# Narrow attention products set singly between feed-forward products, with three other moves in the hand-made order

## The chip, the core and the metric

The kernel runs on one core of one Trainium2 chip. The metric is the device time of one execution in microseconds (us); before the change the median of three runs is 494.69 us (491.87 to 498.25). Engines: PE multiplies matrices (PEld is its weight loading), DVE, ACT and POOL work element by element, SP issues most of the DMA transfers.

## The reference, cut to what matters

For each of 4 batches and 8 heads a recurrent attention runs over 768 positions with 40 values a head; all heads' outputs then go through a feed-forward of 320 -> 2048 -> 320 with a softplus between:

```
C = f*C + i * outer(v, k);  n = f*n + i*k
y = sigmoid(o) * (C @ q) / max(|n . q|, 1)
x = y, all heads of a position side by side      # 3072 x 320
out = softplus(x @ w_in) @ w_out
```

The kernel computes the recurrence in chunks of 128 positions: inside a chunk by products of queries, keys and values, across chunks by the state C and n.

## The kernel before, in words

**Tiles and steps.** 24 steps, one per (batch, chunk), make 8 tiles of 384 positions. The first tile holds chunk 0 of batches 1, 2, 0; the second, the steps (3,0), (0,1) and (0,2); the third, (0,3), (0,4), (0,5). Steps of the first two tiles take the plain way (`plain_step`, L752), the others the wide one (`wide_step`, L804), which sends its result through memory and is not changed.

**Feed-forward.** A block is one slice of 128 of the 2048 hidden columns for one tile: eight products into `hp` (L974, 384 columns), softplus on ACT twice (L848, L849), a difference on DVE (L852), and, two blocks later, nine products into `po` (L942, 320 columns). Blocks 0 to 9 of the first tile come first, then the 16 of the second tile, the last 6 of the first, and the other tiles.

**A plain step.** `scores` (L499) multiplies keys and queries into `sp`, two halves of four heads, and DVE multiplies each by the decays `pw` (L506), which it has scanned (L430) from `fb`, loaded by SP (L421). `inter` (L525) multiplies queries with the old state into `ip`, 8 products of 42 columns, one a head; DVE scales that into `y1` (L531). `values` (L535) multiplies the weighted scores with the values into `yp`, 8 products of 41 columns; DVE adds and divides (L542 to L550) into `x`. `split_x` (L609) transposes `x` on PE into `xp`, ACT casts it into the tile's `X` (L619), and DVE writes the remainder (L621). `state` (L477) makes `cp`, and `new_state` adds it to the state (L486). `ip`, `yp`, `sp`, `xp`, `cp` and the gates' `pg` share one pool of two PSUM buffers (`ps_a`, tag `pa`); a third tile waits until a buffer is read out.

**Gates.** `later_gates` (L142) computes all later chunks' gates once; `pg` (L173) holds their transposes, which ACT copies into `gT` (L179, L180).

**Weights.** Each tensor's chunk is loaded by SP (L221 to L227) into one of three buffers `wr`, brought to float32 by two ACT and two DVE operations (`single`, L190), cast by ACT into the high part (`wih` L236, `woh` L251) and subtracted by POOL into the low part (`wil` L243, `wol` L253). The `wr` buffers also take the queries and keys of every second wide tile (`prepare`, L267).

**Order.** `products` (L923) emits the feed-forward product by product and counts them with `n`; `tick(n)` resumes every generator whose time has come. A generator yields either a time relative to its base, or, below -1000, a distance to the last resumption; `rel` turns a yield of r into such a distance. Engines run their own instructions strictly in the order so written.

Of the kernel before, what the change touches and what calls it, by code (L numbers as in the profile page):

```python
# [39 lines left out]
def mlstm_moe_kernel(  # L40
# [96 lines left out]
        nc.scalar.copy(gT[:, 0, 0, :], pg)  # L137
        yield

    GR = [4, 9, 8, 16, 21, 27]  # L140

    def later_gates():  # L142

        w = S - L
        ig = p1.tile([NCHAIN, w], F32, tag="hiq", name="ig")
        fg = p1.tile([NCHAIN, w], F32, tag="hik", name="fg")
        nc.sync.dma_start(fg, gates[0, :, L:])
        nc.sync.dma_start(ig, gates[1, :, L:])
        yield GR[0]
        m = p2.tile([NCHAIN, w + 1], F32, tag="eg", name="m")  # L150
        nc.vector.tensor_copy(m[:, 0:1], m_end)
        nc.vector.tensor_tensor_scan(m[:, 1:], fg, ig, m[:, 0:1], ALU.add, ALU.max)
        yield GR[0]
        nc.gpsimd.tensor_tensor(fg, fg, m[:, 0:w], op=ALU.add)
        nc.gpsimd.tensor_tensor(fg, fg, m[:, 1:], op=ALU.subtract)
        nc.gpsimd.tensor_tensor(ig, ig, m[:, 1:], op=ALU.subtract)
        yield GR[1]
        nc.scalar.activation(fg, fg, AF.Exp)
        nc.scalar.activation(ig, ig, AF.Exp)
        yield GR[2]  # L160
        d1 = p1.tile([NCHAIN, w], F32, tag="loq", name="d1")
        nc.gpsimd.memset(d1, 0.0)

        nc.vector.tensor_copy(d1[:, 0:w:L], fg[:, 0:w:L])
        nc.vector.memset(fg[:, 0:w:L], 0.0)
        nc.sync.dma_start(fz_d[1:].rearrange("c p s -> p c s"), fg.rearrange("p (c s) -> p c s", s=L))
        fc = d1
        nc.vector.tensor_tensor_scan(fc, fg, d1, 0.0, ALU.mult, ALU.add)
        nc.vector.tensor_copy(fl_s[:, 1:], fc[:, L - 1 : w : L])
        yield GR[3]  # L170
        nc.sync.dma_start(fl_d[:, 1:], fl_s[:, 1:])
        nc.sync.dma_start(fc_d[1:].rearrange("c p s -> p c s"), fc.rearrange("p (c s) -> p c s", s=L))
        pg = ps_a.tile([128, NC + NI - 2, NCHAIN], F32, tag="pa", name="pg")  # L173
        for c in range(1, NC):
            nc.tensor.transpose(pg[:, c - 1], ig[:, (c - 1) * L : c * L], ident[:NCHAIN, :NCHAIN])
        for c in range(1, NI):
            nc.tensor.transpose(pg[:, NC + c - 2], fc[:, (c - 1) * L : c * L], ident[:NCHAIN, :NCHAIN])
        yield GR[4]
        nc.scalar.copy(gT[:, 0, 1:], pg[:, 0 : NC - 1])  # L179
        nc.scalar.copy(gT[:, 1, 1:NI], pg[:, NC - 1 :])  # L180
        yield GR[5]
        nc.sync.dma_start(flast[:, :, 1:], fl_d[:, 1:].partition_broadcast(D))


    wih = cpool.tile([128, 3, DFF], F32R, name="wih")
# [62 lines left out]
    def weights_out(u):  # L248
# [11 lines left out]
        -48, -34, -64, -8, 19, 8, 4, 6, 14, 17, 31, 47, 50, 62, -12, 68, 79, 107, 139,  # L260
    )
    N_LOAD, N_FB, N_SCAN, N_CN, N_VW, N_SIG, N_SP0, N_SP1, N_CP, N_CD, N_IP, N_VI, N_YP, N_X, N_XP = (
        -20, -22, 8, 26, 12, 12, 12, 22, 40, 44, 45, 30, 46, 60, 80,
    )
    OF = [0, 8]

    def prepare(t):  # L267

        yield 0
        parts[t] = []  # L270
        for nm, src in zip("qk", qk[t]):
            lo = (
                stage.tile([D3, H, L], F32R, tag="wr", bufs=WB, name=f"lo{nm}{t}")
                if t % 2
                else p1.tile([D3, H, L], F32R, tag=f"lo{nm}", name=f"lo{nm}{t}")
            )
            nc.sync.dma_start(lo.bitcast(F32), src)
            parts[t].append([lo])
        yield PRD[t > WIDE]
        for (lo,), nm in zip(parts[t], "qk"):  # L280
            hi = p1.tile([D3, H, L], F32R, tag=f"hi{nm}", name=f"hi{nm}{t}")
            nc.scalar.copy(hi, lo.bitcast(F32))
            parts[t]["qk".index(nm)] = hi, lo
            yield -1000 - 5
        for hi, lo in parts[t]:
            for h in range(0, H, 4):
                h2 = slice(h, h + 4)
                nc.gpsimd.tensor_tensor(lo[:, h2], lo[:, h2].bitcast(F32), hi[:, h2], op=ALU.subtract)
                yield -1000 - PSY[t > WIDE]

    PRD, PSY = [40, 78], [8, 12]

    parts = {}
    Xs = {}
# [230 lines left out]
    def inter(z):  # L525
        ip = ps_a.tile([128, H, E2], F32, tag="pa", name=f"ip{z.n}")
        for h in range(H):
            nc.tensor.matmul(ip[:, h, :], z.qst[:, h, :], z.old[:, h, :], start=True, stop=True)
        yield 4
        z.y1 = p1.tile([128, H, E], F32, tag="y1", name=f"y1{z.n}")  # L530
        nc.vector.tensor_tensor(  # L531
            z.y1, ip[:, :, 0:E], gT[:, 1, z.c, z.hs].unsqueeze(2).broadcast_to([128, H, E]), op=ALU.mult
        )

    def values(z):  # L535
        yy = work(z, ps_a, "pa", [128, H, E], "yp", *((ps_a, "pa") if z.s < 2 else (ps_o, "po2")))
        for h in range(H):
            nc.tensor.matmul(yy[:, h, :], z.pws[h // HG][:, h % HG, :], z.vi[:, h, :], start=True, stop=True)  # L538
        yield 4
        if z.c > 0:  # L540
            yp, yy = yy, p1.tile([128, H, E], F32, tag="yy", name=f"yy{z.n}")
            nc.vector.tensor_tensor(yy, yp, z.y1, op=ALU.add)  # L542
        nq = p1.tile([128, H, 1], F32, tag="nq", name=f"nq{z.n}")
        nc.vector.tensor_scalar(nq, yy[:, :, D:E], -1.0, 1.0, op0=ALU.mult, op1=ALU.max)
        nc.vector.tensor_tensor(nq, yy[:, :, D:E], nq, op=ALU.max)
        nc.vector.reciprocal(nq, nq)
        nc.gpsimd.tensor_tensor(z.sig, z.sig, nq.broadcast_to([128, H, D]), op=ALU.mult)
        yield
        z.x = work(z, p1, "x", [128, DM], "x", p2, "gl")
        nc.vector.tensor_tensor(z.x[:, 0:DM].rearrange("p (d h) -> p h d", h=H), yy[:, :, 0:D], z.sig, op=ALU.mult)  # L550
        yield
# [200 lines left out]
    def plain_step(z):  # L752
        if z.s == NG:
            yield 2
            load_values(z)
        else:
            yield N_LOAD
            load(z)
            yield N_FB
            decays(z)  # L760
        yield N_SCAN
        decay(z)
        yield N_VW
        last_decays(z)
        if z.s > NG:
            state_values(z)
        yield N_SIG
        out_gate(z)
        yield N_SP0
        yield from rel(scores(z, 0))  # L770
        yield N_SP1
        if z.s == NG:
            state_values(z)
        yield from rel(scores(z, 1))
        yield N_CN
        old_state(z)
        yield N_VI
        gate_values(z)
        yield N_CP
        state(z)  # L780
        yield N_CD
        c = new_state(z)
        next(c)
        yield N_IP
        next(c)
        if z.c > 0:
            yield from rel(inter(z))
        yield N_YP
        v = values(z)
        for r in v:  # L790
            if not r:
                break
            yield -1000 - r
        yield N_X
        next(v)
        yield N_XP
        yield from rel(split_x(z))

    def rel(g):
        for r in g:  # L800
            if type(r) is int:
                yield -1000 - r
# [85 lines left out]
    def start(g, base):  # L888
        nonlocal order
        order += 1  # L890
        resume(g, base, 0, order)
# [142 lines left out]
    with in_order():  # L1034
        for k, (u, i) in enumerate(tensors[AHEAD:]):
            if k < 2:
                at = (-8, -2)[k]
            else:
                at = (17 - 2 * 34, 26 - 34 + 10 * (u == 4))[i] + 34 * u if u < SPLIT // 2 else (160, 180)[i] + 38 * (u - SPLIT // 2)
            start(convert(u, i), at)  # L1040
            start(fetch(i), at)
        start(first_states(), 0)
        LEAD, TS = 174, 16 * 17
        EARLIER = 26
        before = -1000
        for s in range(NG, NS):
            z = steps[s] = Step(s)
            if z.wide:
                base = TS * z.t - LEAD - EARLIER - TS * (NG - 1 - z.g) // NG if z.t > WIDE else (183, 264, 344)[z.g]
                if z.g == 0:  # L1050
                    start(prepare(z.t), before - 90 if z.t > WIDE else base - 123)
                before = base
            else:
                base = [0, 40, 76][s - NG]
            start(whole(z), base)
        for t in range(WIDE, NT):
            start(wide_gates(t), TS * (t - 1) + GP)
        start(warm_block(4, 5), 0)
        start(warm_block(9, 4), 0)
        start(get_halves(), TS + 17 * SPLIT + 40)  # L1060
        zs = first_tile()
        products()
# [37 lines left out]
```

## Time and profile before

| What | Value |
|---|---|
| Median of three runs | 494.69 us |
| The profiled execution's own time | 498.18 us |
| Its span from first to last instruction | 496.4 us |
| PE busy, PEld busy | 473.1 us (95%), 451.9 us (91%) |
| DVE, ACT, POOL busy | 325.1, 216.6, 222.7 us |
| Mean granted PE clock | 0.979 |
| Moved by DMA | 81.10 MB, mean 163 GB/s |

The sums below are made on the profiled execution, which is 3.5 us above the median. A busy PE row says that products were in the pipeline, not that they followed each other at full pace; where PE stood still, the timeline has the idle time and what ended it in brackets.

### The profile page before, as it was taken

To read this page: it belongs to the slowest core of one execution; us is meant where nothing else is said; L and a number is where in the kernel's file an instruction comes from. 1 tells how busy PE (TensorE), PEld (TensorE's weight loads), DVE (VectorE), ACT (ScalarE), POOL (GpSimd) and SP (SyncE) were. 2 spreads that over 40 slices of the span, in tenths; PEclk is the share of its full clock that TensorE was granted. 3 is DMA by queue.
4 is the path that set the end of the run, shared out by engine and by line. 5 is a ranking of instruction groups with operands and counts; after the bars stand their busy time and mean duration, and the time that the engine had idled before them with its cause. 6 is when DMAs were issued, how large, how long until landed. Compare 5 with 4: busy or idle time off the path is not lost.

```text
span 496.4 us, 9346 instructions
## 1 busy us (share of the span) xinstructions
PE 473.1 (95%) x3444; PEld 451.9 (91%) x3444; DVE 325.1 (65%) x517; ACT 216.6 (44%) x424; POOL 222.7 (45%) x303
## 2 busy tenths in 40 slices
PE   8997899895999999999999999999999999999997
PEld 8986798894998889999999999999999999999996
DVE  7877785689377676695587577578568567542211
ACT  1665544596224632536343534254343632333332
POOL 7375667387656324743355352643384244010000
PEclk9998898899799999999999999999999999999999
DMA  6946895769735877558856684569755572001001
GB/s 191 279 136 171 235 292 168 209 197 207 208 107 138 243 205 205 163 182 209 221 153 180 189 223 149 167 190 213 217 159 174 142 204 89 17 23 41 0 1 40
DMA packets 52991, 81.10 MB, mean 163 GB/s; under 512 B 7906, under 2 KB 31634, under 8 KB 52946
## 3 DMA queue, kind: packets, MB, share of 16 engines
q1 hardware_dynamic: 44738, 67.82, 48.7%
q0 software_dynamic: 4320, 8.26, 6.4%
q10 hardware_dynamic: 3888, 4.43, 2.7%
q8 instruction: 27, 0.44, 0.4%
q14 instruction: 18, 0.15, 0.1%
HBM read 52.38 MB, written 8.80 MB: 123 GB/s over the span
## 4 chain that ended last, share of the span: by engine, by line
PE 75%; DVE 10%; DMA 8%; ACT 3%; issue 2%; SPq 2%; ACTq 0%; DVEq 0%
PE hp L974 33%; PE po L942 31%; PE yq L568 3%; PE sp L504 3%; DVE pw L430 3%; DMA fb<-fz_d 3%; PE cp L481 2%; PE iq L557 2%; DMA lok<-in_qk 2%; DMA wr<-in_w_in 1%; DMA y<-fc_d 1%; DMA vt<-in_vko 1%; PE yp L538 1%; DVE sgo L203 1%; DVE gl L852 1%
## 5 line engine op out<-in xcount | busy, mean ns | idle before, releaser
L974 PE MATMUL hp<-X,wih 128*128 128x384 f32 x768 | 185.1, 345 | 3.0 <-ACT X L619 1.8
L974 PEld LDWEIGHTS hp<-X,wih 128*128 128x128 f32 x768 | 134.4, 191 | 6.1 <-ACT X L619 2.3
L848 ACT ACTIVATE gh<-hp 128x384 fp32r<-128x384 f32 x128 | 62.7, 490 | 175.0 <-PE hp L974 156.3
L852 DVE TENSOR_TENSOR gl<-hp,gh 128x384 fp32r<-128x384 f32 x128 | 70.2, 549 | 60.0 <-ACT hp L849 59.7
L942 PE MATMUL po<-woh,gl 128*128 128x320 f32 x384 | 84.2, 314 | 0.1
L942 PE MATMUL po<-woh,gh 128*128 128x320 f32 x384 | 84.1, 316 | 0.2
L942 PE MATMUL po<-wol,gh 128*128 128x320 f32 x384 | 83.1, 316 | 0.0
L430 DVE TENSOR_TENSOR_SCAN pw<-fb,ident 128x512 f32<-128x512 f32 x48 | 72.5, 1551 | 2.5 <-DMA fb<-fz_d 1.9
L974 PE MATMUL hp<-X,wil 128*128 128x384 f32 x256 | 70.0, 347 | 0.0
L942 PEld LDWEIGHTS po<-woh,gh 128*128 128x128 f32 x384 | 66.0, 190 | 1.6 <-ACT gh L848 0.4
L942 PEld LDWEIGHTS po<-woh,gl 128*128 128x128 f32 x384 | 63.5, 191 | 0.6 <-DVE gl L852 0.4
L942 PEld LDWEIGHTS po<-wol,gh 128*128 128x128 f32 x384 | 62.9, 191 | 1.0 <-issue 0.9
L849 ACT ACTIVATE hp<-hp 128x384 f32<-128x384 f32 x128 | 62.3, 487 | 0.0
L580 POOL DMA_DIRECT2D yd<-y x36 | 20.8, 579 | 89.5 <-DVE y L573 87.7
L974 PEld LDWEIGHTS hp<-X,wil 128*128 128x128 f32 x256 | 46.8, 191 | 1.1 <-issue 1.0
L560 DVE TENSOR_TENSOR y<-iq,y 41x512 f32<-41x512 f32 x36 | 24.5, 682 | 29.9 <-PE iq L557 28.7
L504 PEld LDWEIGHTS sp<-qst,kst 120*128 120x128 f32 (+1 forms) x240 | 33.8, 199 | 9.1 <-DVE sgo L203 5.1
L504 PE MATMUL sp<-qst,kst 120*128 120x128 f32 (+1 forms) x240 | 34.3, 278 | 8.0 <-DMA lok<-in_qk 4.8
L605 ACT CAST X<-eg 128x384 fp32r<-128x384 f32 x18 | 9.2, 513 | 59.2 <-DVE eg L603 59.2
L506 DVE TENSOR_TENSOR pw<-sp,pw 128x512 f32<-128x512 f32 x48 | 31.9, 680 | 4.1 <-PE sp L504 3.8
L486 DVE TENSOR_TENSOR cn<-cn,cp 40x328 f32<-40x328 f32 x16 | 7.8, 486 | 33.9 <-POOL cn L472 31.3
L457 POOL TENSOR_TENSOR vw<-vt,gw 128x328 f32<-128x328 f32 x19 | 16.7, 883 | 27.6 <-DVE gw L451 27.3
(131 smaller groups left out, 602.2 us busy)
## 6 DMA issues: line engine op xcount, KB each, us to landing
fb<-fz_d SPq DMA_DIRECT2D x42, 256.0 KB
vt<-in_vko SPq DMA_DIRECT2D x23, 324.0 KB
qst<-hiq SPq DMA_DIRECT2D x36, 160.0 KB
kst<-hik SPq DMA_DIRECT2D x36, 160.0 KB
wo<-in_w_out SPq DMA_DIRECT2D x8, 640.0 KB
wr<-in_w_in SPq DMA_DIRECT2D x8, 512.0 KB
eg<-in_oT SPq DMA_DIRECT2D x6, 576.0 KB
yd<-y POOLq DMA_DIRECT2D x36, 96.0 KB, 3.5
```

The lines of the kernel that those rows point to most:

```text
L430: nc.vector.tensor_tensor_scan(pw.rearrange(flat), fb.rearrange(flat), ident4.rearrange(flat), 0.0, ALU.mult, ALU.add)
L457: nc.gpsimd.tensor_tensor(z.vw, v1, z.gw.broadcast_to([128, H, E]), op=ALU.mult)
L504: nc.tensor.matmul(sp[:, j, :], z.kst[:, h, :], z.qst[:, h, :], start=True, stop=True)
L506: nc.vector.tensor_tensor(z.pws[i], sp, z.pws[i], op=ALU.mult)
L560: nc.vector.tensor_tensor(y, iq, y, op=ALU.mult)
L568: nc.tensor.matmul(yq[e0:e1, p, :], z.via[:, h * E : h * E + e1 - e0], z.pws[h // HG][:, h % HG, :], start=True, stop=True)
L580: nc.gpsimd.dma_start(rows[i], z.y[i * PP : i * PP + EP])
L848: nc.scalar.activation(gh, hp, AF.Softplus)
L849: nc.scalar.activation(hp, hp, AF.Softplus)
L852: nc.vector.tensor_tensor(gl, hp, gh, op=ALU.subtract)
L942: nc.tensor.matmul(po[j], a[:, j * 128 : (j + 1) * 128], w[:, f, :], start=(first and left[j] == 2), stop=(last and left[j] == 0),)
L974: nc.tensor.matmul(hp, a, r, start=(i == 0), stop=(i == len(seq) - 1))
```

## The change

The 8 `ip` and 8 `yp` products of the second tile's steps are emitted one at a time, with one feed-forward product between two of them. `inter` moves from just ahead of `values` to just behind `gate_values`. The transposes `pg` of the gates and their copies come later and the load of `flast` is written ahead of them. The second half of the scores comes 2 products later (N_SP1), `split_x` 8 products earlier (N_XP). The weight chunks from the sixth on are fetched and converted later, 48 products apart instead of 38, and the fourth tile's queries and keys are loaded later.

```diff
-    GR = [4, 9, 8, 16, 21, 27]
+    GR = [4, 9, 8, 16, 24, 30, 35]
...
         nc.sync.dma_start(fc_d[1:].rearrange("c p s -> p c s"), fc.rearrange("p (c s) -> p c s", s=L))
+        yield GR[4]
+        nc.sync.dma_start(flast[:, :, 1:], fl_d[:, 1:].partition_broadcast(D))
+        yield GR[5]
         pg = ps_a.tile([128, NC + NI - 2, NCHAIN], F32, tag="pa", name="pg")
...
-        yield GR[4]
+        yield GR[6]
         nc.scalar.copy(gT[:, 0, 1:], pg[:, 0 : NC - 1])
         nc.scalar.copy(gT[:, 1, 1:NI], pg[:, NC - 1 :])
-        yield GR[5]
-        nc.sync.dma_start(flast[:, :, 1:], fl_d[:, 1:].partition_broadcast(D))
...
     N_LOAD, N_FB, N_SCAN, N_CN, N_VW, N_SIG, N_SP0, N_SP1, N_CP, N_CD, N_IP, N_VI, N_YP, N_X, N_XP = (
-        -20, -22, 8, 26, 12, 12, 12, 22, 40, 44, 45, 30, 46, 60, 80,
+        -20, -22, 8, 26, 12, 12, 12, 24, 40, 44, 45, 30, 46, 60, 72,
...
-        yield PRD[t > WIDE]
+        yield PRD[min(t - WIDE, 2)]
...
-    PRD, PSY = [40, 78], [8, 12]
+    PRD, PSY = [40, 42, 78], [8, 12]
...
             nc.tensor.matmul(ip[:, h, :], z.qst[:, h, :], z.old[:, h, :], start=True, stop=True)
-        yield 4
+            yield 1 if h < H - 1 else 4
...
             nc.tensor.matmul(yy[:, h, :], z.pws[h // HG][:, h % HG, :], z.vi[:, h, :], start=True, stop=True)
+            if z.s >= NG and h < H - 1:
+                yield 1
...
         gate_values(z)
+        if z.c > 0:
+            yield from rel(inter(z))
         yield N_CP
...
         next(c)
-        if z.c > 0:
-            yield from rel(inter(z))
         yield N_YP
...
-                at = (17 - 2 * 34, 26 - 34 + 10 * (u == 4))[i] + 34 * u if u < SPLIT // 2 else (160, 180)[i] + 38 * (u - SPLIT // 2)
+                at = (17 - 2 * 34, 26 - 34 + 10 * (u == 4))[i] + 34 * u if u < SPLIT // 2 else (168, 192)[i] + 48 * (u - SPLIT // 2)
...
-                    start(prepare(z.t), before - 90 if z.t > WIDE else base - 123)
+                    start(prepare(z.t), (base - 123, before - 54, before - 90)[min(z.t - WIDE, 2)])
```

How this moves instructions is seen at three places. On PE, the `ip` products of step (0,1) before (the trailing number of a name is a running one; `po_0_0` to `po_0_2` are the three output tiles of the first tile):

```order
L974 MATMUL hp_6_793<-X_310,wih 128x384
L528 MATMUL ip_1_796<-cn_0_523,qst_0_121 128x42 x8
L974 MATMUL hp_6_793<-X_310,wih 128x384 x3
L504 MATMUL sp_0_2_815<-qst_0_131,kst_0_132 128x128 x4
L974 MATMUL hp_6_793<-X_310,wil 128x384
L538 MATMUL yp_1_823<-vi_1_735,pw_1_0_649 128x41 x4
L538 MATMUL yp_1_823<-vi_1_735,pw_1_1_651 128x41 x4
L974 MATMUL hp_6_793<-X_310,wil 128x384
```

and with the change:

```order
L977 MATMUL hp_5_726<-X_310,wih 128x384 x3
L529 MATMUL ip_1_737<-cn_0_515,qst_0_121 128x42
L977 MATMUL hp_5_726<-X_310,wih 128x384
L529 MATMUL ip_1_737<-cn_0_515,qst_0_121 128x42
L977 MATMUL hp_5_726<-X_310,wil 128x384
L618 MATMUL xp_0_746<-ident_79,x_0_700 128x128 x2
L620 MATMUL xp_0_746<-ident_79,x_0_700 64x128 x2
L529 MATMUL ip_1_737<-cn_0_515,qst_0_121 128x42
L977 MATMUL hp_5_726<-X_310,wil 128x384
L529 MATMUL ip_1_737<-cn_0_515,qst_0_121 128x42
```

The run of eight is taken apart, stands one block earlier, and the transposes `xp` of step (3,0) fall into it. On ACT, the cast of step (0,2) into the second tile's `X`, before:

```order
L848 ACTIVATE gh_9_1019<-hp_9_1004 128x384
L849 ACTIVATE hp_9_1004<-hp_9_1004 128x384
L251 CAST woh<-sgo_1017 128x640
L198 ACTIVATE magi_1039<-wr_757 128x640
L201 ACTIVATE sgi_1041<-wr_757 128x640
L619 CAST X_761<-xp_2_1043 128x3x128
```

and with the change:

```order
L851 ACTIVATE gh_9_1019<-hp_9_1004 128x384
L852 ACTIVATE hp_9_1004<-hp_9_1004 128x384
L622 CAST X_745<-xp_2_1028 128x3x128
L252 CAST woh<-sgo_1017 128x640
L851 ACTIVATE gh_0_1059<-hp_0_1043 128x384
```

The cast goes ahead of three operations on weights. On SP's queue, around the last loads of step (0,4) (`kst`, `qst` from `lok`, `loq`), before:

```order
L405 DMA vt_4_1238<-in_vko 128x648
L227 DMA wo_1242<-in_w_out 128x2x640
L390 DMA kst_4_1233<-lok_704 40x1024
L390 DMA qst_4_1232<-loq_702 40x1024
L492 DMA cn_3_1192<-cn_3_1192 40x336
L493 DMA cn_3_1192<-cn_3_1192 40x336
L277 DMA loq_1344<-in_qk 120x1024
L277 DMA lok_1346<-in_qk 120x1024
```

and with the change:

```order
L406 DMA vt_4_1233<-in_vko 128x648
L391 DMA kst_4_1228<-lok_704 40x1024
L391 DMA qst_4_1227<-loq_702 40x1024
L228 DMA wo_1275<-in_w_out 128x2x640
L493 DMA cn_3_1183<-cn_3_1183 40x336
L494 DMA cn_3_1183<-cn_3_1183 40x336
L422 DMA fb_5_0_1406<-fz_d 128x512
L422 DMA fb_5_1_1408<-fz_d 128x512
```

One weight load of 640 KB no longer stands ahead of them, and the fourth tile's loads (480 KB each) come four issues later than shown. Elsewhere on DVE, the second product L506 of step (0,1) goes behind a weight operation (L203) that stood after it; the scans L430 of step (0,3) go ahead of two weight operations that stood before them; and on ACT the copies of the first half result (`ob0h`, L999) stay behind the casts of `wih` that wait for those two.

## Rows read from the trace of the kernel before

**Rows 1.** The page's first lines: span, PE's busy time, and the clock granted to PE in 40 slices of 12.4 us, in tenths of full speed.

```profile
span 496.4 us, 9346 instructions
...
PE 473.1 (95%) x3444; PEld 451.9 (91%) x3444; DVE 325.1 (65%) x517; ACT 216.6 (44%) x424; POOL 222.7 (45%) x303
...
PEclk9998898899799999999999999999999999999999
```

**Rows 2.** What PE waited for in the first 200 us, a part: waiting engine, tile and line, what came last, us in total, times, longest.

```profile
PE sp L504 <- DMA lok<-in_qk: 4.8, 1, 4.8
...
PE hp L974 <- ACT X L605: 1.2, 1, 1.2
PE sp L504 <- issue: 0.9, 1, 0.9
```

**Rows 3.** Stretches of 10 us: length, then busy us (instructions) of PE, PEld, DVE, ACT, POOL, the granted PE clock, the DMA engines' busy share, GB/s.

```profile
40.00:50.00 10.00, 9.07 (x70) 8.42 (x71) 6.44 (x13) 5.92 (x15) 5.15 (x6) 0.83 0.82 224
...
70.00:80.00 10.00, 9.29 (x76) 8.42 (x75) 8.63 (x14) 6.93 (x13) 5.92 (x6) 1.00 0.69 217
80.00:90.00 10.00, 9.90 (x51) 9.90 (x52) 4.65 (x10) 2.60 (x5) 7.18 (x8) 0.66 0.61 181
...
120.00:130.00 10.00, 5.40 (x20) 5.43 (x21) 6.76 (x9) 3.85 (x8) 9.17 (x10) 0.69 0.87 212
...
200.00:210.00 10.00, 10.00 (x79) 9.65 (x78) 6.64 (x10) 5.03 (x10) 7.89 (x12) 1.00 0.55 154
```

**Rows 4.** PE's timeline around the gates' transposes and step (3,0)'s values: start us, us, line, instruction, count, and in brackets the idle time ahead with what ended it.

```profile
40.93 0.30 PE L177 MATMUL pg<-ident,d 32*128 32x32 f32 x2 [2.73 <-DVE d L168]
...
46.01 0.60 PE L942 MATMUL po<-woh,gh 128*128 128x320 f32 x3
...
50.10 0.45 PE L942 MATMUL po<-wol,gh 128*128 128x320 f32 x2
50.39 1.87 PE L538 MATMUL yp<-vi,pw 128*128 128x41 f32 x16
52.09 0.39 PE L942 MATMUL po<-wol,gh 128*128 128x320 f32 x1
52.32 0.60 PE L942 MATMUL po<-woh,gl 128*128 128x320 f32 x3
52.76 0.52 PE L974 MATMUL hp<-X,wih 128*128 128x384 f32 x2
...
58.04 1.30 PE L504 MATMUL sp<-qst,kst 128*128 128x128 f32 x8 [2.25 <-DVE pw L506]
```

**Rows 5.** The timelines of ACT, POOL, SP's queue (SPq) and DVE, one after the other: what those products and the wait at 58.04 hang on. Columns as in rows 4.

```profile
41.82 0.72 ACT L251 CAST woh<-sgo 128x640 fp32r<-128x640 f32 x1 [4.17 <-DVE sgo L205]
...
42.69 1.55 POOL L253 TENSOR_TENSOR wol<-sgo,woh 128x640 fp32r<-128x640 f32 x1 [3.48 <-ACT woh L251]
...
47.18 0.90 SPq L421 DMA_DIRECT2D fb<-fz_d  x2
...
53.40 2.80 DVE L430 TENSOR_TENSOR_SCAN pw<-fb,ident 128x512 f32<-128x512 f32 x2 [1.87 <-DMA fb<-fz_d]
...
57.29 0.69 DVE L506 TENSOR_TENSOR pw<-sp,pw 128x512 f32<-128x512 f32 x1
```

**Rows 6.** PE's timeline at the narrow products of steps (0,1) and (0,2) and at the start of the third tile.

```profile
65.61 1.87 PE L528 MATMUL ip<-cn,qst 128*128 128x42 f32 x16
...
69.56 1.98 PE L538 MATMUL yp<-vi,pw 128*128 128x41 f32 x16
...
80.10 1.98 PE L528 MATMUL ip<-cn,qst 128*128 128x42 f32 x16 [0.81 <-DVE cn L486]
...
82.69 3.34 PE L538 MATMUL yp<-vi,pw 128*128 128x41 f32 x16
...
94.06 1.22 PE L974 MATMUL hp<-X,wih 128*128 128x384 f32 x4 [1.47 <-ACT X L619]
95.12 0.51 PE L974 MATMUL hp<-X,wil 128*128 128x384 f32 x2
```

**Rows 7.** The timelines of DVE and then ACT at what those stretches wait for.

```profile
60.41 0.68 DVE L506 TENSOR_TENSOR pw<-sp,pw 128x512 f32<-128x512 f32 x1
62.06 1.20 DVE L203 SCALAR_TENSOR_TENSOR sgo<-wo,sgo 128x640 uint32<-128x640 uint32 x1 [0.96 <-ACT sgo L201]
...
80.35 0.56 DVE L621 TENSOR_TENSOR X<-xp,X 128x384 fp32r<-128x384 f32 x1 [0.30 <-ACT X L619]
...
98.18 3.38 DVE L430 TENSOR_TENSOR_SCAN pw<-fb,ident 128x512 f32<-128x512 f32 x2
...
93.55 0.46 ACT L619 CAST X<-xp 128x384 fp32r<-128x384 f32 x1
```

**Rows 8.** PE's timeline: the last products of the first half result, and steps (0,3) and (0,4) of the third tile.

```profile
101.68 1.26 PE L942 MATMUL po<-woh,gh 128*128 128x320 f32 x3
...
115.47 1.08 PE L568 MATMUL yq<-pw,vi 128*64 128x128 f32 x16 [1.53 <-DVE y L560]
...
124.60 1.08 PE L504 MATMUL sp<-qst,kst 120*128 120x128 f32 x4 [4.83 <-DMA lok<-in_qk]
```

**Rows 9.** SP's queue ahead of the last of those: when it issued the loads.

```profile
110.23 0.39 SPq L227 DMA_DIRECT2D wo<-in_w_out  x1
...
111.92 0.73 SPq L390 DMA_DIRECT2D qst<-loq  x1
```

## Prediction, made before the change was run

> **What bounds the kernel now.** I began with the page's first lines and the clock by slices [rows 1]: PE is busy 95% of a 496.4 us span, and its clock is below full only in the first dozen slices of 12.4 us. DVE, ACT and POOL stand at 65% and less. So PE bounds the kernel, and a gain must be one of three: less PE work, less idle PE, or a higher clock. The work stays the same. The table by stretches [rows 3] tells where the other two lie: at 200 to 210 us PE is busy 10.00 of 10.00 at clock 1.00, and nothing can be had from such stretches except by removing work. The low clocks are at 40 to 50 (0.83), 80 to 90 (0.66) and 120 to 130 (0.69). A granted clock between 0.5 and 1 is a mixture of the two levels, 1.2 and 2.4 GHz, so I price what a stretch lost as (1 - granted) x its 10 us: 1.7, 3.4 and 3.1 us. Last, the list of waits [rows 2] and PE's timeline [rows 4, 6, 8] name the idle pieces, and the timelines of DVE, ACT and SP [rows 5, 7, 9] what ended them. The largest is a wait of 4.83 us for a load [rows 8].
>
> **The change part by part.** Minus is a gain, in us of the profiled execution.
>
> *a, gates' transposes later.* The idle 2.73 ahead of `pg` at 40.93 goes [rows 4]. What is late next: the out products at 46.01 need `woh`, cast until 42.54, and `wol`, ready at 44.24 [rows 5]; and PE stops at the second scores in any case, until 58.04, since these hang on the `fb` load issued at 47.18 on a queue where it does not move, then the scan at 53.40 and the product that ends at 57.98 [rows 5]. So most of the 2.73 comes back as a longer wait there. What remains is the two products that N_SP1 moves into that wait. Three products of an output block took 52.76 - 52.32 = 0.44, or 0.147 each [rows 4]: **-0.3**. Were the load chain sooner too, it would be -2.7.
>
> *b, the alternation itself.* 16 `ip` and 24 `yp` products are set singly. The run of 16 records (8 products, two passes each) at 50.39 was followed at 52.09, and the one product after it took 0.23 [rows 4]: (1.70 + 0.23 - 0.147) / 16 = 0.111 a pass. No row shows one narrow product between two block products. Lower end: a weight load hides under the block product, 40 x 0.111 = -4.4. Upper end: every return to block products costs what it costs after the run, 35 returns more x (0.23 - 0.147) = +2.9. I take **0**: the nearest row, the exit from the run, shows a narrow product's missing cover paid at the next product, so what is gained on one side is paid on the other.
>
> *c, `ip` on its own and spread.* `ip` no longer waits for `cn` at 80.10: -0.8 [rows 6]. But a spread `ip` holds one of the two PSUM buffers longer, and what needs the other now waits for it. `xp` of step (3,0) needs the buffer that the product L506 reads out; that stands now behind L203, which ends at 63.26, so it ends 0.68 later, at 63.94 [rows 7]. PE gets there, by the order, some 20 products ahead of where the run stood: 65.61 - 20 x 0.147 = 62.7 [rows 6]. Wait +1.2. `cp` of step (0,2) needs the buffer that the write of `X` ends with, 80.91 [rows 7]; PE was ready at 80.10 - 0.81 = 79.3 [rows 6] and has three products ahead of it, 79.7: wait +1.2. Net **+1.6**; bounds -0.8 (no wait) and +4 (both twice as long).
>
> *d, the clock at 80 to 90.* The low stretch followed the idle 0.81, the run `ip` of 1.98 and the run `yp` of 3.34 [rows 6]. With block products between them I expect no fall: **-3.0** of the 3.4 lost [rows 3]. Bounds 0 and -3.4.
>
> *e, `X` sooner.* The third tile's first product waited 1.47 for ACT's cast, which ended at 94.01 [rows 6, 7]. In the new order it stands ahead of three operations on weights: **-1.5**.
>
> *f, the first half result.* Its copies stand on ACT behind casts that wait for DVE, now behind the two scans of 3.38 [rows 7]. The three products at 101.68 took 1.26, where three without a wait took 0.60 (46.01) [rows 4, 8]: a wait of about 0.65 is there already. It grows at most to the scans less this group, 3.38 - 1.26 = 2.1: **+1.4**; lower end 0.
>
> *g, `yq` of step (0,3)* waited 1.53 for DVE [rows 8]; ACT has less weight work ahead of it, a part of the wait goes: **-0.4**, bounds 0 and -1.5.
>
> *h, scores of step (0,4).* They waited 4.83, until 124.60 [rows 8]. The row names `lok`, but the products read `kst` and `qst`, and the last of their loads was issued at 111.92, behind a weight load at 110.23 [rows 9]. This weight load goes: its 128 x 2 x 640 values of 4 bytes, 0.655 MB, are 3.1 us at the 212 GB/s of this stretch [rows 3], an estimate. Terms a to g add up to -2.2, so loads are issued that much sooner and land at 124.6 - 2.2 - 3.1 = 119.3, while PE comes at 124.60 - 4.83 - 2.2 = 117.6. Wait 1.7 in place of 4.83: **-3.1**. Of the clock lost there (3.1) half, **-1.5**; bounds 0 and -3.1.
>
> The later conversions of the weight chunks go to engines and queues that are not the bound past 131 us; the fourth tile's loads come later, into stretches with less DMA (share 0.55 against 0.87 [rows 3]): 0.
>
> Sum -0.3 + 0 + 1.6 - 3.0 - 1.5 + 1.4 - 0.4 - 3.1 - 1.5 = -6.8. The profiled execution took 498.18, 3.5 above the median of 494.69: 491.4 profiled, **488** as a median.
>
> **The rivals.** *A, the sum above*: 488, chance 0.50; its own range 482 to 493 (the bounds of b to h, not all at one end).
>
> *B, loads hide.* Each narrow product's weights come in under the block product, and nothing is paid at the return: 488 - 4.4 = 483.5. Against it speaks the 0.23 at 52.09 [rows 4]. Chance 0.12. The Trainium skill, page "TensorE: Matmul & The Clock Gate", section "Step-by-step: what each phase is for", says that the engine pulls a weight load ahead into a background buffer while the present product streams. By that rule the first pass of each single narrow product would have its load for nothing, which is this rival; the row after the run does not bear it out fully.
>
> *C, transfers set the pace.* At 120 to 130 the DMA engines are busy 0.87 of the time [rows 3], the loads land at 124.6 - 3.1 = 121.5 whatever PE gained before, and the clock falls there again: only 3.1 is kept, 498.2 - 3.1 - 3.5 = 491.6. The list of loads ahead of step (0,4) is otherwise the same, which speaks for it; that they are issued when PE's products get there speaks against it. Chance 0.24.
>
> *D, slower: the ring of two PSUM buffers.* The spread `ip` makes PE stop in the middle of narrow work, as in c, and the clock falls behind each stop. Then d's 3.0 is not had, another 3.4 is lost as at 80 to 90 [rows 3], DVE's scans for the next steps start about 2.8 later (one scan pair, [rows 5]), and h's 4.6 goes, since loads are issued later: -6.8 + 3.0 + 3.4 + 2.8 + 4.6 = +7.0, or 501.7. It decides if `xp` of step (3,0) starts more than about 1.5 us behind the product ahead. For it: the idle 0.81 at 80.10 was such a wait, and the low stretch followed it. Against: that wait's own place is cleared. Chance 0.14. The Trainium skill, same page, section "A second HAM failure mode: psum-queue depth-cycling", describes a kernel whose clock oscillates because PE pauses briefly between groups while PSUM buffers cycle. It would make this rival likelier than I put it; no row here shows an oscillation from pauses as short as 0.81 alone.
>
> **How the numbers follow.** Range 480 to 497: B with h's clock wholly kept (483.5 - 1.6) and f's +1.4 absent is 480.5; C with b's upper end is 494.5, and D's milder half, one stop without the lost loads, is 501.7 - 4.6 = 497.1. About 2 in 10 stay outside, mostly D. Two per cent, about what a measurement of this kernel can tell from no change, are 484.8 and 504.6. Faster by more: most of B, 0.10, a third of A, 0.17, a little of C, 0.03: 0.30. Slower by more: part of D, 0.06. Within: 0.64.
>
> **What would show it.** In the changed profile: no gap ahead of `pg`, a wait of 3 to 4 us at the second scores of (0,1) (a); `xp` of (3,0) behind about 1 us of idle (c); clock 1.00 at 80 to 90 (d); the third tile's first product without a wait for `X`, some 3 us sooner (e); `po` waiting about 2 us at the half result's copies (f); scores of (0,4) waiting 2 us or less, with a clock between 0.69 and 1 (h). It would be wrong if the clock stayed low at 40 to 130 in spite of shorter waits, or if single products cost clearly more or less than 0.222 each beyond what the blocks take.

## The result, and the profile after

The median of 20 runs is 498.51 us, that of 20 runs of the kernel before 495.37: ratio 1.0069, 95% interval 1.0048 to 1.0091. The change is 0.7% slower, outside the predicted range of 480 to 497. Medians and ratios here and below leave out executions in a slower state, of which a few sets had some (two of six with N_SP1 back, two of twelve with the late loads alone). The profiled execution took 501.5 us with a span of 499.4, 3.0 longer than before. A profile is one execution among many that differ (497.36 to 501.5 for the change, 491.41 to 500.5 for the kernel before), so what a part is worth is read from the ratios, and where it arises from the profiles.

The most useful reading is how far the same feed-forward product lies behind its place in the trace of before. There are 2176 of them on PE, in the same order in both traces; the table gives the start of some, from the two traces, in us. A minus means that the changed kernel is ahead.

```
product   before    after   lag
     20    43.66    38.74  -4.92
     60    55.34    56.71  +1.37
     70    61.43    60.06  -1.37
     80    64.74    69.58  +4.84
    120    78.85    85.80  +6.95
    140    90.00    90.82  +0.82
    260   118.08   118.64  +0.56
    280   129.53   123.52  -6.01
    340   142.22   137.63  -4.59
    360   146.35   148.45  +2.10
    520   179.16   180.09  +0.93
    540   184.85   188.09  +3.24
   2000   464.77   468.02  +3.25
```

Large steps between products 100 and 140 mean little, since the narrow work between them changed places, and so does the lead at product 20, where only the kernel before had already waited for the gates' transposes. After product 540 nothing more happens, and the lag of 3.25 is the result. The kernel was 4.6 us ahead at product 340 and lost 6.7 in the next twenty.

The list of PE's waits after (waiting engine, tile and line, what came last, us in total, times, longest), which answers to [rows 2]; the 4.83 us wait ahead of step (0,4) stood there before:

```profile
PE sp L505 <- DMA y<-fc_d: 4.3, 1, 4.3
PE po L945 <- ACT cn L489: 3.1, 1, 3.1
PE xp L618 <- DVE pw L507: 3.0, 1, 3.0
...
PE hp L977 <- ACT X L608: 1.9, 1, 1.9
```

The stretches after, columns as in [rows 3], the clock third from the end:

```profile
40.00:50.00 10.00, 6.88 (x39) 5.86 (x38) 7.91 (x14) 5.85 (x14) 7.47 (x7) 0.71 0.83 228
60.00:70.00 10.00, 7.04 (x35) 6.12 (x33) 4.67 (x8) 5.17 (x10) 4.87 (x5) 0.73 1.01 265
...
80.00:90.00 10.00, 9.19 (x78) 8.35 (x78) 5.31 (x11) 4.86 (x10) 8.73 (x8) 1.00 0.47 149
120.00:130.00 10.00, 8.09 (x64) 7.52 (x63) 8.77 (x12) 5.09 (x11) 8.55 (x8) 1.00 0.61 151
140.00:150.00 10.00, 6.28 (x24) 6.31 (x25) 7.19 (x8) 2.57 (x5) 7.75 (x8) 0.66 0.79 195
180.00:190.00 10.00, 8.09 (x42) 7.53 (x41) 9.04 (x15) 2.64 (x6) 4.72 (x8) 0.83 0.91 237
```

The low clocks of 80 to 90 (0.66 before) and 120 to 130 (0.69) are gone. 60 to 70 is lower than before, and new ones stand at 140 to 150 and 180 to 190. Those at 40, 60 and 140 stand behind the three long stops in PE's timeline, 3.12, 2.96 and 4.28 us, which hold most of the kernel's losses; the 0.54 at 120.86 is what is left of the wait of (0,4). Columns as in [rows 4]:

```profile
43.60 0.74 PE L945 MATMUL po<-woh,gh 128*128 128x320 f32 x3 [3.12 <-ACT cn L489]
...
60.46 0.42 PE L977 MATMUL hp<-X,wil 128*128 128x384 f32 x1
63.84 0.44 PE L618 MATMUL xp<-ident,x 128*128 128x128 f32 x2 [2.96 <-DVE pw L507]
...
120.86 0.63 PE L505 MATMUL sp<-qst,kst 120*128 120x128 f32 x4 [0.54 <-DVE gl L855]
...
143.72 1.08 PE L505 MATMUL sp<-qst,kst 120*128 120x128 f32 x4 [4.28 <-DMA y<-fc_d]
```

*At 64 us.* DVE's timeline shows what `xp` waited for: the product that frees a PSUM buffer stood behind a weight operation, and that waited 1.55 us for ACT.

```profile
62.35 0.82 DVE L204 SCALAR_TENSOR_TENSOR sgo<-wo,sgo 128x640 uint32<-128x640 uint32 x1 [1.55 <-ACT sgo L202]
63.10 0.68 DVE L507 TENSOR_TENSOR pw<-sp,pw 128x512 f32<-128x512 f32 x1
```

*At 143 us.* The scores of step (0,5) had to wait for loads, as those of (0,4) had before. The row names `y`, but the scores read `kst` and `qst`. The landing times in the traces settle it: the last part of `qst` landed at 143.42, 0.3 us before these scores, and at 124.29 in the kernel before, 0.3 us before those of (0,4). SP's queue after: the fourth tile's queries and keys (`loq`, `lok` from `in_qk`, 480 KB each) are issued ahead of this step's (`kst`, `qst`).

```profile
126.89 0.40 SPq L278 DMA_DIRECT2D loq<-in_qk  x1
127.39 0.34 SPq L278 DMA_DIRECT2D lok<-in_qk  x1
...
132.04 1.20 SPq L391 DMA_DIRECT2D kst<-lok  x1
133.29 0.73 SPq L391 DMA_DIRECT2D qst<-loq  x1
```

From the issue at 133.29 to the first scores it took 10.4 us. In the kernel before, the fourth tile's loads stood at 116 us, behind the loads of (0,4) [rows 9], and the scores of (0,5) began without a wait (SP's queue, then PE):

```profile
116.08 0.36 SPq L277 DMA_DIRECT2D loq<-in_qk  x1
...
143.88 0.56 PE L504 MATMUL sp<-qst,kst 120*128 120x128 f32 x4
```

### The profile page after: what moved, and what is told of

Read it like the earlier page. It is cut to its first block, busy times and chain, and to the rows that moved or that the text cites. A ratio compares the mean times of both kernels' runs of the same rounds, so it can differ in the third digit from the quotient of the medians.

```text
span 499.4 us, 9348 instructions
## 1 busy us (share of the span) xinstructions
PE 473.6 (95%) x3444; PEld 452.2 (91%) x3444; DVE 322.9 (65%) x517; ACT 217.1 (43%) x424; POOL 217.5 (44%) x303
## 4 chain that ended last, share of the span: by engine, by line
PE 76%; DVE 7%; DMA 6%; ACT 4%; issue 4%; POOL 1%; ACTq 0%; SPq 0%; POOLq 0%; DVEq 0%
PE hp L977 31%; PE po L945 30%; PE sp L505 4%; PE yq L571 3%; PE cp L482 2%; DMA kst<-hik 2%; DMA wo<-in_w_out 2%; PE iq L560 1%; PE yp L539 1%; PE fb L417 1%; DVE pw L431 1%; DMA y<-fc_d 1%; DVE sgi L204 1%; DVE sgo L204 1%; DMA out<-ob 1%
## 5 line engine op out<-in xcount | busy, mean ns | idle before, releaser
L945 PE MATMUL po<-woh,gh 128*128 128x320 f32 x384 | 86.1, 319 | 4.3 <-ACT cn L489 3.1
L977 PE MATMUL hp<-X,wil 128*128 128x384 f32 x256 | 71.1, 349 | 0.0
```

The lines of the kernel that those rows point to most:

```text
L945: nc.tensor.matmul(po[j], a[:, j * 128 : (j + 1) * 128], w[:, f, :], start=(first and left[j] == 2), stop=(last and left[j] == 0),)
L977: nc.tensor.matmul(hp, a, r, start=(i == 0), stop=(i == len(seq) - 1))
```

## The experiments

Theory: two places cost what the change gained, the stop at 64 us (one operation's place on DVE) and the loads that now stand ahead of step (0,5). Main rivals: the two PSUM buffers stop PE whatever DVE does, and the DMA engines as a whole set the pace. All times below are medians, and ratios to the kernel before, run on the same chip; the change itself stands at 1.0069.

**Undoing one part each.** First, the fourth tile's loads early again:

```diff
-    start(prepare(z.t), (base - 123, before - 54, before - 90)[min(z.t - WIDE, 2)])
+    start(prepare(z.t), (base - 123, before - 90, before - 90)[min(z.t - WIDE, 2)])
-    PRD, PSY = [40, 42, 78], [8, 12]
+    PRD, PSY = [40, 78, 78], [8, 12]
```

> The changed kernel with the fourth tile's queries and keys loaded as early as before (their issue back ahead of the loads of step (0,5) by some 36 products); all else of the change kept. Theory (the wait of step (0,4) was not saved but handed on: 0.98 MB now stand just ahead of step (0,5)'s own loads): the 4.28 us wait of the (0,5) scores at 143.72 goes or falls below 1, the clock at 143 to 150 is 1.00, the scores of (0,4) still don't wait, and the kernel is 5 to 7 us faster than with the change, 491.5 to 493.5. Rival (the DMA engines as a whole set the pace, and the same bytes have to pass ahead of 143 us either way): a wait of 3 us or more stays at (0,4) or (0,5), with a low clock behind it, and the time is 497 to 500.

Measured 498.07, ratio 1.0012 (0.9982 to 1.0042). The theory did not come out: the wait was split. PE stopped 2.71 us at (0,4) and 2.02 at (0,5), each with a clock of 0.83 in its stretch. The time is in the rival's range, though the ratio is 0.6% below the change's and the intervals do not meet. The loads that leave one step's way stand in the other's.

Second, N_SP1 from 24 back to 22:

```diff
-        -20, -22, 8, 26, 12, 12, 12, 24, 40, 44, 45, 30, 46, 60, 72,
+        -20, -22, 8, 26, 12, 12, 12, 22, 40, 44, 45, 30, 46, 60, 72,
```

> The changed kernel with N_SP1 back at 22, so that the product L507 of step (0,1) stands ahead of the weight operation L204 on DVE again; all else of the change kept. Theory (the 2.96 us stop ahead of the transposes xp at 63.84, and the half clock from 64 to 71 behind it, come from this one place in DVE's order): the stop falls below 1 us, the clock at 60 to 70 is above 0.9, and the kernel is 3 to 6 us faster than with the change, 492.5 to 495.5. Rival (the spread ip holds one of two PSUM buffers, and xp stops whatever DVE does first): the stop stays above 2 us, 497.5 to 499.5.

Measured 491.36, ratio 0.9893 (0.9859 to 0.9927): the theory, with a little more gain than it said. DVE's and then PE's timeline of this kernel:

```profile
61.40 0.68 DVE L507 TENSOR_TENSOR pw<-sp,pw 128x512 f32<-128x512 f32 x1
63.05 0.83 DVE L204 SCALAR_TENSOR_TENSOR sgo<-wo,sgo 128x640 uint32<-128x640 uint32 x1 [0.97 <-ACT sgo L202]
```

```profile
62.14 0.44 PE L618 MATMUL xp<-ident,x 128*128 128x128 f32 x2 [0.32 <-DVE pw L507]
...
138.66 1.09 PE L505 MATMUL sp<-qst,kst 120*128 120x128 f32 x4 [3.79 <-DMA y<-fc_d]
```

The stop fell from 2.96 to 0.32, the clock at 60 to 70 rose to 1.00. A two-product shift, counted in the prediction as 0.3 us of gain in term a and 1.2 of loss in term c, was worth a loss of 1.8% by the ratios, some 8.7 us. In the two profiles the difference is 4.3 us at product 140 and 7.7 at the end; 2.3 of the rest is the wait for `X` at 183 us with its low clock, which is shorter here (1.11) and has none. The wait at (0,5) is still there: this kernel was 9.2 us ahead of before at product 340 and 3.0 at product 360.

Third, the gates' transposes back (the three pieces of `later_gates` in the diff, and GR, as before):

> The changed kernel with the gates' transposes, their copies and the load of flast where they were before; all else of the change kept. Theory (PE's stop at 40 us belongs to the chain of the decay scan, sgo on DVE and woh on ACT, and the move of the transposes only changes which product stands behind it): about 2.7 us of idle come back ahead of pg, the 3.12 ahead of the out products goes, and the time is within 1.5 us of the change's, 497 to 500. Rival (the moved transposes lengthened the stop or the half clock from 44 to 51 us): 2 to 4 us faster, 494.5 to 496.5.

Measured 497.12, ratio 1.0001 (0.9973 to 1.0029). The profile agrees with the theory: 2.7 us of idle ahead of `pg` and none ahead of the out products, and at product 60 the lag is 0.75 where the change has 1.37. But that profile took 500.69 us, the slowest of the twelve. The median is in the theory's range, while the ratio lies 0.7% below that of the change, some 3.4 us where the profile shows 0.6, and the intervals do not meet, which is the rival's; a run below with the same part back speaks the other way.

Fourth, the products of a step in runs again, where the change starts them:

```diff
-            yield 1 if h < H - 1 else 4
+        yield 4
...
-            if z.s >= NG and h < H - 1:
-                yield 1
```

> The changed kernel with the eight ip and eight yp products of a step emitted as one run again, at the places where the change starts them; all else of the change kept. Theory (single products cost PE nothing of themselves, and they keep the clock up at 80 to 90 us): the clock at 80 to 90 falls below 0.8, and the kernel is 1 to 4 us slower than with the change, 499.5 to 502.5, if the stop at 64 us stays. Rival (each return to the block products costs 0.08 us, and the spread run is what holds the PSUM buffers): the stop at 64 us goes and the kernel is 3 to 6 us faster, 492.5 to 495.5.

Measured 494.61, ratio 0.9934 (0.9901 to 0.9967). The clock at 80 to 90 stayed at 1.00 with runs, so single products did not mend it. The stop at 64 us shrank to 1.63, since PE reaches `xp` later when the run stands whole ahead of it. The time is the rival's: with the products in runs the kernel is 1.35% faster than with single ones, clear of noise. Its one reason, a spread run that holds a buffer, fits the shorter stop; its other, the cost at each return, is not there. In the changed kernel's own timeline a feed-forward product and a narrow one beside it took 0.40:

```profile
72.35 0.42 PE L977 MATMUL hp<-X,wih 128*128 128x384 f32 x1
72.61 0.31 PE L539 MATMUL yp<-vi,pw 128*128 128x41 f32 x2
72.75 0.42 PE L977 MATMUL hp<-X,wih 128*128 128x384 f32 x1
...
78.14 0.86 PE L977 MATMUL hp<-X,wih 128*128 128x384 f32 x4
78.85 0.34 PE L977 MATMUL hp<-X,wil 128*128 128x384 f32 x1
```

Four feed-forward products alone took 78.85 - 78.14 = 0.71, 0.18 each; what is left is 0.22 for the narrow product, 0.11 a pass, the price in a run.

**What the loads hang on, and the place of `ip`.** N_SP1 at 22, and the fourth tile's loads behind those of (0,5):

```diff
-    start(prepare(z.t), (base - 123, before - 54, before - 90)[min(z.t - WIDE, 2)])
+    start(prepare(z.t), (base - 123, before - 12, before - 90)[min(z.t - WIDE, 2)])
```

> The changed kernel with N_SP1 back at 22 and the fourth tile's loads issued another 42 products later, behind step (0,5)'s own loads on SP's queue. Theory (what is left of the wait at the (0,5) scores, 3.8 us beside N_SP1 at 22, and the half clock behind it come from those 0.98 MB standing ahead): the wait goes below 1 us, the clock at 130 to 150 is 1.00, and the time is 4 to 6 us below that of N_SP1 alone, 486.5 to 489. Rival (other transfers fill the time ahead of step (0,5) as well, or the late loads make the fourth tile wait): a wait of 2 us or more stays there or opens at the fourth tile, 491 to 494.

Measured 489.52, ratio 0.9868 (0.9825 to 0.9910): faster than both kernels, a little short of the theory's time. Against N_SP1 alone (0.9893) the intervals overlap widely, so what the late loads add to it is not clear of noise. SP's queue and the stretch of this kernel:

```profile
126.57 0.72 SPq L391 DMA_DIRECT2D qst<-loq  x1
...
129.46 0.44 SPq L278 DMA_DIRECT2D loq<-in_qk  x1
```

```profile
130.00:140.00 10.00, 10.00 (x71) 9.76 (x68) 9.13 (x14) 3.32 (x8) 4.35 (x5) 1.00 0.96 217
140.00:150.00 10.00, 10.00 (x77) 9.49 (x77) 6.21 (x11) 4.64 (x11) 4.91 (x6) 1.00 0.55 171
```

PE is busy without a gap at 130 to 150, and the scores of (0,5) began at 133.29, 6.7 us after their last load was issued, against 10.4. That load landed at 133.10, only 0.2 us before: there was nothing to spare, and that no stop shows is partly luck. The DMA share at 130 to 140 is 0.96: the engines carry no less, only in another order. That speaks against a common pace and for the order in the queue. A wait of 1.94 us stands next, at 152.61, ahead of the first scores of the fourth tile.

The weight chunks as early as before:

```diff
-    (168, 192)[i] + 48 * (u - SPLIT // 2)
+    (160, 180)[i] + 38 * (u - SPLIT // 2)
```

> The changed kernel with the late weight chunks fetched and converted as early as before (160, 180 and every 38 products); all else of the change kept. Theory (the (0,4) wait of 4.83 us went because a 640 KB weight load no longer stands ahead of its loads): a wait of 2 us or more is back at the scores of (0,4) near 120 us with a low clock behind it, the wait of (0,5) shrinks by as much, and the time is within 3 us of the change's, 497 to 501.5. Rival (the wait went because all loads were issued sooner): no wait at (0,4), 497 to 499.

Measured 497.73, ratio 1.0062 (1.0025 to 1.0100), the first case: a wait of 2.02 at (0,4) with a clock of 0.83 at 120 to 130, and 1.15 at (0,5). The list of waits names an operation on DVE for the 2.02, but `qst` landed at 123.48, 0.3 us before the scores at 123.78. The `wo` load stands at 112.72, ahead of the step's last loads at 114.22 and 115.00. Before, the wait was 4.83; the rest of it had another source, which the last run below shows.

`inter` back at its old place, products single:

```diff
         gate_values(z)
-        if z.c > 0:
-            yield from rel(inter(z))
...
         next(c)
+        if z.c > 0:
+            yield from rel(inter(z))
         yield N_YP
```

> The changed kernel with inter back at its old place just ahead of values, its products still single; all else of the change kept. Theory (the stop ahead of xp at 63.84 is the product L507 behind L204 on DVE, and the place of ip adds no more than a buffer that is held): a stop of 1 us or more stays near 64, and the time is within 2 us of the change's, 496.5 to 500.5. Rival (ip standing apart is what makes the ring of two PSUM buffers stop PE): no stop over 1 us at 60 to 66, clock above 0.95 at 60 to 80, 493 to 496. On the clock at 80 to 90: if ip standing apart is what kept it at 1.00, it falls below 0.9; if single products did, it stays.

Measured 499.68, ratio 1.0090 (1.0053 to 1.0128). The time is the theory's, and so is a stop near 64. It stands ahead of another instruction that needs a PSUM buffer, `cp` (PE, then DVE):

```profile
63.89 0.78 PE L482 MATMUL cp<-vw,vt 128*40 128x41 f32 x16 [1.45 <-POOL wih L246]
```

```profile
63.11 0.68 DVE L507 TENSOR_TENSOR pw<-sp,pw 128x512 f32<-128x512 f32 x1
```

The row names an operation on POOL that had ended at 63.50; the product on DVE, still behind the weight operation, ended at 63.79, just before, and the next run has the same (1.44 at 64.42, the product's end at 64.32). No low clock followed (1.00 at 60 to 70). So, as far as these times tell, the place of DVE's product alone makes a stop of 1.45 us; with `ip` standing apart and a buffer in its hand it is 2.96, with half clock behind it. Further stops follow: 3.85 us ahead of `xp` at 80.48, with 0.83 at 80 to 90, and 4.47 at (0,5).

The same with runs as well (both edits above together):

> The changed kernel with inter back at its old place and its products and those of yp in runs again, so that of the change only the transposes, N_SP1, N_XP, the weight chunks and the fourth tile's loads are left. Theory (the low clock at 80 to 90 us before came from the idle 0.81 and the two long runs close together, and is mended by the place of ip, not by single products): the clock at 80 to 90 falls below 0.8. Rival (it came from something else that the change moved): it stays at 1.00. Time by the first 494.5 to 499, by the second 491 to 495.

Measured 497.24, ratio 1.0016 (0.9988 to 1.0044). The time is the theory's. Against single products at the same place (1.0090) it is 0.7% faster, clear of noise. At 80 to 90 the clock is 1.00, as the rival has it, but the low stretch has only moved:

```profile
70.00:80.00 10.00, 9.29 (x45) 9.29 (x46) 8.06 (x15) 5.34 (x9) 5.11 (x7) 0.66 0.49 157
80.00:90.00 10.00, 10.00 (x86) 9.42 (x85) 4.52 (x11) 3.73 (x8) 7.83 (x9) 1.00 0.55 185
```

It stands behind a wait of 1.18 for `y1` at 70.71. With `ip` at its old place there is a low stretch between 70 and 90 in all three kernels (before, and these two); with it apart none at 80 to 90, in runs or singly.

**Three combinations.** The late loads alone (the edit of the fifth run, N_SP1 at 24):

> The changed kernel with only the fourth tile's loads issued another 42 products later, behind step (0,5)'s own; N_SP1 stays 24. Theory (two independent losses: the loads ahead of (0,5), and the stop at 64 us; with the first mended the second shows in full): no wait over 1 us at the (0,5) scores, the 2.96 us stop at 64 and its half clock stay, and the time is 3 to 6 us above that of both mended (489.5), 492.5 to 495.5. Rival (once PE loses 6 us at 64, the loads have time to land, and mending them gains nothing): 497 to 499.

Measured 496.54, ratio 1.0003 (0.9968 to 1.0039). The stop at 64 stays (2.96, clock 0.70) and no wait is left at (0,5), as the theory has it. The time lies between the theory's and the rival's: by the ratios 0.7% below the change, clear of noise, about half of what the theory said. In this profile half clock behind the stop at 64 went on longer (0.62 at 70 to 80, where the change has 0.93). A new wait of 2.87 us opens at 162.24, ahead of the fourth tile's first scores, with 0.83 at 160 to 170. The wait has been handed on once more, to the step that uses the late loads.

With the gates' transposes back as well (N_SP1 at 22, late loads):

> The changed kernel with N_SP1 at 22, the fourth tile's loads late, and the gates' transposes back where they were before. Theory (moving the transposes cost about 1 us at 40 to 51 by a longer half clock and gave nothing): 0.5 to 1.5 us below the same kernel with the transposes moved, 488 to 489. Rival (the move frees PE for later work): 490 to 492.

Measured 493.95, ratio 0.9932 (0.9897 to 0.9967), slower than without, and slower than both expectations. At product 60 this kernel stood 0.70 behind before, the other 0.96, so at the transposes themselves they hardly differ. It then waited 2.53 at (0,4) where the other waited 1.35. Whether moving the transposes helps thus depends on what comes after, and stays open.

The kernel before with late loads alone (the same distances put into it):

> The kernel before, with only the fourth tile's loads issued 78 products later, behind step (0,5)'s own. Theory (the 4.83 us wait of (0,4) before had two parts, the 640 KB weight load ahead of its loads and the 0.98 MB issued just behind them, which share the DMA engines): the wait of (0,4) falls to between 1.5 and 3.5, no wait over 1 us opens at (0,5), and the kernel is 2 to 5 us faster than before. Rival (loads issued behind others don't slow them): the (0,4) wait stays above 4, no change in time.

Measured 495.64, ratio 0.9968 (0.9933 to 1.0003). The wait of (0,4) fell from 4.83 to 1.60 and its clock rose to 1.00, though these loads had been issued after that step's own, and no wait over 1 us opened at (0,5), as the theory has it. The theory's gain in time did not come: the interval includes no change. For 2.78 us of wait and a clock of 0.66 came at 160 to 170, ahead of the fourth tile's first scores:

```profile
160.59 1.09 PE L504 MATMUL sp<-qst,kst 120*128 120x128 f32 x4 [2.78 <-DMA y<-fc_d]
```

## Why the prediction was wrong, point by point

Two steps failed: the stop at 64 us, too small in term c and without its clock, and the fourth tile's loads, put at nothing. Undone together (the fifth run) they bring the ratio to 0.9868, where the forecast was 488 / 494.69 = 0.9865. That this is so close is partly luck, since other terms were off too; of the two, N_SP1 is worth 1.8% undone alone, the late loads 0.7%.

- *Term h and the line behind it* failed. The scores of (0,4) did better than forecast, a wait of 0.54 for 1.7 and a clock of 1.00. But the fourth tile's loads "come later, into stretches with less DMA: 0" was a step that failed: they came just ahead of step (0,5), whose scores had not waited before, and cost 4.28 us and 3.4 of clock (0.66 over 10 us) in this profile. The share that I quoted was that of 200 to 210 us; the loads went to 127. Rival C had the mechanism, with the wrong step and without its full price.
- *Term c* was mis-sized. The end of the product on DVE came at 63.78 (forecast 63.94), but PE was there at 60.88, not 62.7: 2.96 us instead of 1.2, and a stop of that length was followed by half clock (0.73 at 60 to 70, 0.93 at 70 to 80, 3.4 us in all), which the term left out. Undoing N_SP1 took the stop away. This is rival D's mechanism at the place and beyond the point (1.5 us) that it named. Of D's prices the clock behind the stop came; d's gain was not lost, nor that at (0,4).
- *Term a*: the gap ahead of `pg` went, but did not come back at 58. It came ahead of the out products, 3.12 us: the first tile's `cp` lies in `po`'s PSUM buffers (`work`, L318), and the copy that frees one stood on ACT behind `woh`, which waited for DVE behind the gates' scan (L168) as `pg` had. At the second scores all this had come out even, 57.96 against 58.04, as forecast. But the wait there was 0.50 and not the 3 to 4 us that were to show it, and no half clock followed it, as one had before (0.88 at 60 to 70). So at product 70, where -0.3 was forecast, the lag was -1.37, with a first product of `ip` already done. This lead is most of why PE stood at `xp` sooner than term c had it.
- *Term b* was right for the product alone: 0.22, neither gain nor cost. The Trainium skill's rule named beside rival B (page "TensorE: Matmul & The Clock Gate", section "Step-by-step: what each phase is for"), a weight load pulled ahead under a running product, shows no gain in time here: 0.11 a pass, in a run or singly. The load itself is pulled ahead in this trace, as the rule has it (PEld begins with that of the narrow product of 72.61 at 72.43, under the block product of 72.35). What the term left out is what a spread `ip` or `yp` does to the stops: at either place of `ip` the kernel with runs was faster, by 1.35% and 0.7%.
- *Term d*: the size was right (clock 1.00 at 80 to 90), by luck, for the reason was wrong. Not the block products between but the place of `ip` did it.
- *Terms e, f, g*: the wait for `X` fell from 1.47 to two of 0.4; the wait at the half result's copies was 1.17 (forecast 2.1), that of `yq` 0.9 (forecast 1.1).
- *Not forecast*: a wait of 1.91 for `X` at 183, 1.17 before, with 0.83 at 180 to 190, about 2.3 us between products 520 and 540. It is missing from some of the experiments' profiles, and its cause was not tried.

## What to carry to other kernels

When a wait for a load goes, look for the next step on the same queue whose operands are now the last to land, and price any load that was moved by what it is issued ahead of. Where a narrow product holds one of two PSUM buffers for longer, the operation that frees the other must not stand behind anything that can wait, on its own engine. A term that contains a stop of some microseconds on PE needs the half-clock stretch behind it as a second term, with a range, since here the same stop of 2.96 us cost between 3.4 and 6.8 us of clock. Before products are set singly for the clock's sake, the same order with runs should be measured.

## What the runs showed of the hardware

Stops of 2.96 to 4.3 us on PE were followed by half clock for 6 to 7 us in the changed kernel. At 64 us (two-us stretches of its table, columns as above):

```profile
64.00:66.00 2.00, 2.00 (x12) 1.66 (x12) 1.26 (x2) 0.48 (x1) 0.02 (x1) 0.66 1.01 244
66.00:68.00 2.00, 2.00 (x10) 2.00 (x10) 0.00 (x0) 0.80 (x2) 0.00 (x0) 0.50 1.03 256
68.00:70.00 2.00, 2.00 (x9) 1.67 (x8) 0.96 (x2) 2.00 (x4) 1.15 (x1) 0.50 1.02 294
```

PE was busy throughout these, but at 0.50, one of the two levels. How long it lasts is not fixed: behind the same stop of 2.96 us the stretch 70 to 80 had 0.93 in the changed kernel, 0.82 and 0.80 in the first and sixth run and 0.62 with the late loads alone. Nor does the length of the stop alone decide it: 1.91 us at 183 in the changed kernel was followed by 0.83 at 180 to 190, 1.94 at 152.61 in the fifth run by 1.00 at 150 to 170.

A load issued behind another can slow it: in the kernel before, (0,4)'s scores began 12.7 us after the issue of their last load (111.92 to 124.60), with the 0.98 MB behind it taken away 9.9 us (113.36 to 123.28). The landings say the same, 12.4 and 9.6 us after the issue.
